# A third key buffer part, and one load for the second pair's keys, in a decode step of attention and MLP

## The chip, the cores and the metric

The kernel runs on one core of a Trainium2 chip. The time is device time in microseconds (us), from one launch; lower is better. A core has TensorE (PE, matmuls into the banks of PSUM), VectorE (DVE), ScalarE (ACT), GpSimd (POOL) and SyncE (SP, which here issues the transfers). Sixteen DMA engines carry the transfers between HBM and the on-chip memory SBUF, which has 128 partitions.

## The reference

One token (batch 1, sequence 1, width 512, bf16) goes through an attention block with a cache and then through an MLP block.

```
xn = layernorm(x)
q  = (xn @ wq) as 32 heads of 128
scores = q @ k_cache / sqrt(128)     # k_cache: 8 KV heads x 16384 positions x 128, 4 query heads per KV head
p  = softmax(scores);  o = p @ v_cache
h  = x + o @ wo
B(y): c  = gelu(layernorm(y) @ w1), four column groups shifted along the sequence, @ w2
      x1 = y + c
      return x1 + gelu(layernorm(x1) @ w3) @ w4
out = h + B(layernorm(h))
```

With a sequence of one token every shift by one or two positions brings in zeros, so w1 and w2 do not contribute and the kernel does not load them. k_cache and v_cache are 32 MB each, wq and wo 4 MB each, w3 and w4 1.75 MB each.

## The kernel before

Two KV heads form a pair; there are four pairs (PAIRS, 0 to 3). One pair's keys are 8 MB: 128 rows (partitions) of 64 KB; its values are as large. In SBUF `kb` holds one pair's keys, 64 KB per partition in two parts of 32 KB (`kb[0]`, `kb[1]`, the two halves of a pair); `vb` holds one pair's values, and wq before that. The weights wo go into `kb[0]`, w3 and w4 into `kb[1]`, once pair 3's keys have been used.

The chain of one pair: DVE transposes the first half of the keys from `kb` into `kt` (32 KB per partition) in blocks of 32x32 (L656), then the second half; PE multiplies each piece of `kt` with the queries `qn` into two banks of scores (L667); DVE takes the maximum (L681), PE and DVE make the bias from it, ACT writes exp of the scores into `p_sb` (L693), DVE transposes that into `pt` (L697), and PE multiplies `pt` with the values (L708). `kt` is reused piece by piece: a transpose of the second half waits until PE has read that piece of the first half. After pair 3 come the sum over heads, the product with wo (L794), the layernorm, w3 (L819), the gelu, w4 (L845) and the output's transfer.

What orders the work: every operation is appended to its engine's list in the order of the code and waits on semaphores for the operations that it depends on. Dependencies are named by keys. `("r", part, i)` stands for a key part: a load of the part writes it, so it waits until the transposes that read the part are done; `("kt", piece)` stands for a piece of the transposed keys; `"pt"` for the transposed probabilities. All large loads are issued by SyncE, in its list's order, and a load that waits holds up those behind it on that list. The values of the next pair are loaded into `vb` when PE has finished the pair's products (L708). The keys of the next pair are loaded by `load_keys(j, y)`: pairs in WHOLE in one load of 64 KB rows, the others in two loads of 32 KB rows, one for each half. CUTS and LAST cut the transposes of a half into pieces (five for a pair, nine for pair 3).

Of the kernel before, what the change touches and what calls it, by code (L numbers as in the profile page):

```python
# [349 lines left out]
D = 512  # L350
# [35 lines left out]
def bass_sequential_preLN__gqa_block_cached__mixer_s_mlp__decode_kernel(  # L386
# [13 lines left out]
    with ExitStack() as ctx:  # L400
# [30 lines left out]
        qcol = sb("qcol", [128, 4, PAIRS * REP, 32], FP32)  # L431
# [11 lines left out]
        osum = sb("osum", [128, D], FP32)  # L443
# [4 lines left out]
        hr = sb("hr", [128, 128], FP32)  # L448
        hx = sb("hx", [128, 128], FP32)
        rs = [sb(f"rs{i}", [128, 2], FP32) for i in range(2)]  # L450
        hc = sb("hc", [128, NCH, 32], BF16)
        xs = sb("xs", [128, 128], FP32)
        hg = sb("hg", [128, FQ], BF16)
        hT = sb("hT", [128, NCH, 32], FP32)
        hcol = sb("hcol", [128, NHC, 32], BF16)
        fin = sb("fin", [64, 256], BF16)
# [16 lines left out]
        def load(name, dst, src, key, by="SP", also=()):  # L473
            P.op(by, lambda e: e.dma_start(dst, src), w=[key, *also], dma=name)  # L474
# [12 lines left out]

        def load_values(j):
# [14 lines left out]
        def dve(fn, r=(), w=(), bank=(), own=None):  # L503
            return P.op("DVE", fn, r, w, bank, own=own)
# [24 lines left out]
        def piece(cuts, m):  # L529
            return [lo <= m < hi for lo, hi in cuts].index(True)  # L530
# [120 lines left out]
        def pieces(x, t, n):  # L651
            return x[:, :].rearrange("p (x l) -> p x l", x=2)[:, :, t * KP:(t + n) * KP]

        def transpose_keys(y, cuts):
            for t, n in zip(cuts, [b - a for a, b in zip(cuts, [*cuts[1:], 8])]):
                P.op("DVE", lambda e, t=t, n=n: e.transpose(pieces(kt, t, n).bitcast(I32), pieces(kb[y], t, n).bitcast(I32)),  # L656
                     r=[("r", y, i) for i in range(RPARTS)], w=[("kt", t + i) for i in range(n)], worth=n)
# [92 lines left out]
        for j in range(PAIRS):  # L750
            P.part()
            clear()
            P.part("query", j)
            dve(lambda e, j=j: e.tensor_copy(qn[:, :, :], qb[:, :, j, :]), r=["qb", ("s", 0), ("s", 1)], w=["qn"])
# [21 lines left out]
        act(lambda e: e.activation(scr[0:1, 1:2], mean4[0:1, 0:1], ACTF.Gelu_apprx_tanh), r=["mean4"], w=["scr"])  # L776
        for n, (lo, hi) in enumerate(WO):
            load(f"wo{n}", wo_sb[:, lo * D:hi * D], A_wo.rearrange("(p r) c -> p (r c)", p=128)[:, lo * D:hi * D],
                 ("r", 0, n))
        w3_in = B_w3.rearrange("(p k) f -> p k f", p=128)  # L780
        for n, (lo, hi) in enumerate(W3):
            load(f"w3{n}", w3_sb[:, lo:hi, :], w3_in[:, lo:hi, :], ("r", 1, n))
        w4_in = B_w4.rearrange("(p m) c -> p m c", p=128)
        for n, (lo, hi) in enumerate(W4):
            load(f"w4{n}", w4_sb[:, lo:hi, :], w4_in[:, lo:hi, :], ("r", 1, len(W3) + n))
# [4 lines left out]
        dve(lambda e: e.tensor_copy(o_b[:, :], o_f[:, :]), r=["o_f", ("r", 0, 0)], w=["o_b"])  # L790

        for r_ in range(32):
            q = r_ % 4
            pe(lambda e, r_=r_, q=q: e.matmul(O_ps[0][32 * q:32 * q + 32, :], copies(o_b[:, r_:r_ + 1], 32),  # L794
                                              wo_sb[:, r_ * D:(r_ + 1) * D], start=(r_ < 4),
                                              stop=(r_ < 4 or r_ >= 28), skip_group_check=(r_ >= 4)),
               r=["o_b"] + [("r", 0, n) for n in (piece(WO, r_),) if n], w=[("O", 0)], bank=[("O", 0)],
               times=None if r_ else 4, many=4)
        for n in range(2):
            unread(None)  # L800
# [4 lines left out]
        for q in range(4):  # L805
# [4 lines left out]
        S = ("st", 1)  # L810
        row_sums(1, h_ps, hkey)
        act(lambda e: e.activation(hc[:, :, :], hT[:, :, :], ACTF.Identity, bias=s[:, 0:1], scale=1.0),
            r=["hT", (S, 0)] + [("r", 1, 0)], w=["hc"])
        unread(4)


        for k in range(NCH):
            for q in range(4):
                pe(lambda e, k=k, q=q: e.matmul(s_ps[32 * q:32 * q + 32, 0, 0:FQ], hc[:, k, :],  # L819
                                                w3_sb[:, k, q * FQ:(q + 1) * FQ], start=(k == 0), stop=(k == NCH - 1)),  # L820
                   r=["hc"] + [("r", 1, n) for n in (piece(W3, k),) if n], w=[("s", 0)], bank=[("s", 0)])
# [5 lines left out]
        for n in range(2):  # L827
            lo, hi = n * NHC // 2, (n + 1) * NHC // 2
            act(lambda e, lo=lo, hi=hi: e.activation(
                hg[:, :].rearrange("p (i m) -> p i m", m=NHC)[:, :, lo:hi],  # L830
                s_ps[:, 0, 0:FQ].rearrange("p (i m) -> p i m", m=NHC)[:, :, lo:hi],
                ACTF.Gelu_apprx_tanh, scale=s[:, 7:8]), r=[("s", 0), (S, 7)], w=[("hg", n)], bank=[("s", 0)])
            dve(lambda e, lo=lo, hi=hi: e.transpose(
                hcol[:, lo:hi, :].rearrange("p m u -> p (m u)"),
                hg[:, :].rearrange("p (i m) -> p m i", m=NHC)[:, lo:hi, :]), r=[("hg", n)] + [("r", 1, len(W3))] * (n == 0), w=[("hcol", n)])
        for m in range(NHC):
            if m == 4:
                pe(None)
            if m == NHC - 1:
                for o in range(4):  # L840
                    pe(lambda e, o=o: e.ldweights(hcol[:, NHC - 1, :], tile_position=(0, 32 * o)), r=[("hcol", 1)])
            for o in range(4):
                pe(lambda e, m=m, o=o: held(
                    e, h_ps[32 * o:32 * o + 32, 0:128], hcol[:, m, :], w4_sb[:, m, o * 128:(o + 1) * 128], True)
                    if m == NHC - 1 else e.matmul(  # L845
                    h_ps[32 * o:32 * o + 32, 0:128], hcol[:, m, :], w4_sb[:, m, o * 128:(o + 1) * 128],
                    start=False, stop=False, skip_group_check=True),
                   r=[("hcol", 2 * m // NHC)] + [("r", 1, len(W3) + n) for n in (piece(W4, m),) if n],
                   w=[hkey], bank=[hkey])


# [38 lines left out]
```

## Time and profile before

| | before |
|---|---|
| time, median of 3 runs (lowest to highest) | 189.6 us (189.44 to 189.7) |
| span of the profiled execution, first to last instruction | 188.3 us |
| granted TensorE clock, mean over the span | 0.916 |
| bytes read from HBM | 79.17 MB, 420 GB/s over the span |
| key loads | 4 of 4 MB (32 KB rows), 2 of 8 MB (64 KB rows) |
| value loads | 4 of 8 MB |

The profiled execution's own time is its span; it leaves out what lies ahead of the first and behind the last instruction. If that execution took the median's time, this is 1.3 us. In the rows of the profile a line number is one of the code above, "out<-in" names the tiles, "x" counts instructions, and what stands behind an arrow in brackets ended the engine's idle time. SPq marks SyncE's issue of a transfer, which is not the transfer itself: "us to landing" runs from the issue to the last byte's arrival being told.

### The profile page before, as it was taken

The page shows a single profiled execution, that of the slowest core. Times are in us where ns is not written, and L with a number is a line of the kernel's source. Part 1 is how long each engine was busy: PE and PEld are TensorE (multiplying, and loading weights), DVE is VectorE, ACT ScalarE, POOL GpSimd, SP SyncE. Part 2 cuts the span into 40 slices and gives each one's busy share as a digit, 9 for nine tenths or more (in the row PEclk, how much of TensorE's full clock was granted, in tenths as well). Part 3 has the DMA queues.
Part 4 walks back from the last instruction along what each step waited for, and adds up shares of the span by engine and source line. Part 5 has one row for each costly group of instructions (what it writes and reads, how often), then busy time and mean ns, then how long its engine had stood idle before and what let it go on. Part 6 is the DMA issues. An engine that isn't in the chain of part 4 may idle for free.

```text
span 188.3 us, 2375 instructions
## 1 busy us (share of the span) xinstructions
PE 124.1 (66%) x760; PEld 48.3 (26%) x761; DVE 115.8 (62%) x138; ACT 13.7 (7%) x21; POOL 4.6 (2%) x8
## 2 busy tenths in 40 slices
PE   0109700698979978897910019799799889775772
PEld 0104200233322522332500003333244333222221
DVE  5730741999636998936300069993699898633173
ACT  3000200000004000004000000000400000500012
POOL 8100000000000000000000000000000000000000
PEclk9999985569999999999995557999999999999999
DMA  7999999999799999987999999998999996999994
GB/s 252 445 418 445 445 445 446 445 445 445 334 445 446 445 557 418 418 390 334 446 445 445 445 446 445 445 445 334 445 446 445 543 390 292 445 432 411 433 429 193
DMA packets 2607, 79.19 MB, mean 421 GB/s; under 512 B 302, under 2 KB 430, under 8 KB 686
## 3 DMA queue, kind: packets, MB, share of 16 engines
q1 hardware_dynamic: 2598, 79.17, 98.0%
q8 instruction: 1, 0.02, 0.0%
q10 hardware_dynamic: 8, 0.00, 0.0%
HBM read 79.17 MB, written 0.00 MB: 420 GB/s over the span
## 4 chain that ended last, share of the span: by engine, by line
DMA 69%; DVE 23%; PE 4%; issue 3%; SPq 1%; DVEq 0%
DMA kb<-in_A_k_cache_dram 54%; DVE kt L656 22%; DMA kb<-in_B_w_dram 15%; PE banks L667 3%; SPq L474 1%; PE banks L845 0%; DVE fin L852 0%; DVEq L147 0%; DVE den L725 0%; PE banks L524 0%; DVE od L723 0%; SPq L147 0%
## 5 line engine op out<-in xcount | busy, mean ns | idle before, releaser
L667 PE MATMUL banks<-kt,qn 128*128 x256 | 68.1, 401 | 36.8 <-DVE kt L656 35.7
L656 DVE STREAM_TRANSPOSE kt<-kb 128x2048 int32<-128x2048 int32 (+2 forms) x24 | 70.6, 2994 | 27.5 <-DMA kb<-in_A_k_cache_dram 26.4
L667 PEld LDWEIGHTS banks<-kt,qn 128*128 x256 | 25.4, 100 | 79.4 <-issue 65.5
L518 PE MATMUL banks<-qb 128*128 128x512 bf16 x61 | 22.1, 387 | 0.7 <-issue 0.2
L708 PE MATMUL banks<-vb,pt 128*32 128x512 bf16 x256 | 14.7, 379 | 1.1 <-POOLq L500 1.1
L693 ACT ACTIVATE p_sb<-banks,bias 128x1024 bf16<-128x1024 f32 x4 | 4.5, 1114 | 133.3 <-DVE nmh L688 133.3
L632 PE MATMUL banks<-vb,xn 128*128 x32 | 8.5, 432 | 6.7 <-DVE xn L623 6.7
L697 DVE STREAM_TRANSPOSE pt<-p_sb 64x1024 bf16<-64x1024 bf16 x8 | 9.9, 1239 | 4.4 <-ACT p_sb L693 4.3
L681 DVE TENSOR_REDUCE mx<-banks 128x1 f32<-128x1024 f32 x4 | 4.9, 1224 | 10.5 <-PE banks L667 10.5
L518 PEld LDWEIGHTS banks<-qb 128*128 128x128 bf16 x62 | 5.9, 97 | 16.0 <-issue 15.7
L708 PEld LDWEIGHTS banks<-vb,pt 128*32 128x32 bf16 x256 | 8.5, 97 | 5.4 <-POOLq L500 1.2
L639 DVE STREAM_TRANSPOSE qcol<-banks 64x1024 f32<-64x1024 f32 x4 | 4.8, 1227 | 6.7 <-PE banks L632 6.7
L632 PEld LDWEIGHTS banks<-vb,xn 128*128 128x128 bf16 x32 | 3.5, 108 | 11.4 <-issue 8.7
L676 ACT ACTIVATE banks<-mean 128x1024 f32<-128x1024 f32 x4 | 4.1, 1027 | 18.6 <-DVE qcol L639 18.5
L684 PE MATMUL banks<-mxd,mean 128*128 128x128 f32 x8 | 2.0, 326 | 4.7 <-DVE mxd L682 4.7
L732 DVE SCALAR_TENSOR_TENSOR od<-banks,rowc,od 128x128 f32<-128x128 f32 x12 | 4.2, 350 | 0.4
L794 PE MATMUL banks<-kb,o_b 128*32 128x512 bf16 x44 | 3.3, 384 | 1.6 <-DVE o_b L790 1.1
L729 DVE TENSOR_SCALAR od<-banks,rowc 128x128 f32<-128x128 f32 x4 | 1.3, 319 | 4.6 <-PE banks L708 4.6
L603 PE MATMUL banks<-x,quarter 4*128 4x128 bf16 x1 | 0.3, 286 | 5.4 <-DVE quarter L601 5.4
L601 DVE CAST quarter<-ident_f 4x128 bf16<-4x128 f32 x1 | 2.9, 2901 | 1.3 <-DMA x<-in_A_x_dram 1.3
L737 PE MATMUL banks<-od,zo 128*32 128x128 f32 x10 | 2.0, 283 | 1.8 <-DVE od L732 1.6
L803 DVE COPY osum<-banks 128x256 f32<-128x256 f32 x2 | 0.8, 418 | 4.0 <-PE banks L794 4.0
(74 smaller groups left out, 39.5 us busy)
## 6 DMA issues: line engine op xcount, KB each, us to landing
kb<-in_A_k_cache_dram SPq DMA_DIRECT2D x4, 4096.0 KB, 20.5
vb<-in_A_wq_dram SPq DMA_DIRECT2D x1, 3584.0 KB, 11.7
kb<-in_A_wo_dram SPq DMA_DIRECT2D x1, 2560.0 KB, 26.2
kb<-in_B_w_dram SPq DMA_DIRECT2D x1, 1792.0 KB, 24.4
kb<-in_A_wo_dram SPq DMA_DIRECT2D x1, 1536.0 KB, 29.5
kb<-in_B_w_dram SPq DMA_DIRECT2D x1, 1024.0 KB, 26.6
kb<-in_B_w_dram SPq DMA_DIRECT2D x1, 640.0 KB, 27.7
vb<-in_A_wq_dram SPq DMA_DIRECT2D x1, 512.0 KB, 3.6
```

The costliest lines, as they stand in the source:

```text
L518: P.op("PE", lambda e: e.matmul(O_ps[1][:, :], field[:, 0:128], field[:, 0:512], start=True, stop=True), r=["qb"], bank=[("O", 1)], times= ...
L632: pe(lambda e, k=k: e.matmul(row[:, bass.ds(P.b + P.b0, 512)], copies(xn[:, k:k + 1], 128), wq_k[:, k, bass.ds(P.c + P.c0, REP * DH)], sta ...
L639: dve(lambda e, g=g, b=b, half=half: e.transpose(qcol[64 * g:64 * g + 64, 2 * b:2 * b + 2, :, :].rearrange("p e m u -> p (e m u)"), half.r ...
L656: P.op("DVE", lambda e, t=t, n=n: e.transpose(pieces(kt, t, n).bitcast(I32), pieces(kb[y], t, n).bitcast(I32)), r=[("r", y, i) for i in ra ...
L667: pe(lambda e, n=n: e.matmul(row[:, bass.ds(P.y, 512)], qn[:, n, bass.ds(P.q, 128)], key_piece(P.k, n), start=False, stop=(n == 3), skip_g ...
L676: act(lambda e: e.activation(s_all, copies(mean4[:, 0:1], 1024), ACTF.Identity, scale=0.0), r=["mean4", "p"], w=[("s", 0), ("s", 1)], **both)
L681: dve(lambda e: e.tensor_reduce(mx[:, :], s_all, AX.X, ALU.max), r=[("s", 0), ("s", 1)], w=["mx"], **both)
L693: act(lambda e: e.activation(p_sb[:, :], s_all, ACTF.Exp, bias=bias[:, 0:1], scale=float(SCALE), accum_out=acc[:, :]), r=[("s", 0), ("s", ...
L697: dve(lambda e, g=g: e.transpose(pt[64 * g:64 * g + 64, :, :, g, :], p_sb[64 * g:64 * g + 64, :]), r=["p"], w=["pt"])
L708: pe(lambda e, l=l, ct=ct, ch=ch: e.matmul(O_ps[0][32 * ct:32 * ct + 32, :], pt[:, l, ch, :, :].rearrange("p g u -> p (g u)"), tiles[:, l ...
L732: dve(lambda e, block=block, c=c: e.scalar_tensor_tensor(od[:, :], block, rowc[:, c:c + 1], od[:, :], ALU.mult, ALU.add), r=[key, "rowc", ...
L794: pe(lambda e, r_=r_, q=q: e.matmul(O_ps[0][32 * q:32 * q + 32, :], copies(o_b[:, r_:r_ + 1], 32), wo_sb[:, r_ * D:(r_ + 1) * D], start=(r ...
```

## The change

`kb` gets a third part of 32 KB per partition. Pair 1's keys are now loaded whole, as pairs 0 and 2 are, and a table AT tells in which two neighbouring parts a whole load lands: pair 0 in parts 1 and 2, pair 1 in parts 0 and 1, pair 2 in parts 1 and 2. Pair 3's keys are still loaded by halves, into parts 0 and 1. The weights wo go into part 2, w3 and w4 into part 0. To make room, ten tiles that live only before, between or after the uses of `kt` become regions of `kt`: qcol, p_sb, osum, hg, hcol, fin, hc, hr, xs and hT. Since p_sb now lies in `kt`, the first key transpose of a pair also waits for `"pt"`, that is, for the operations that last wrote `pt`.

```
-WHOLE = (0, 2)
+WHOLE = (0, 1, 2)
+AT = (1, 0, 1)
...
-        p_sb = sb("p_sb", [128, 1024], BF16)
...
-        kb_all = sb("kb", [128, 256 * DH], BF16)
-        kb = [kb_all[:, i * 128 * DH:(i + 1) * 128 * DH] for i in range(2)]
+        kb_all = sb("kb", [128, 3 * 128 * DH], BF16)
+        kb = [kb_all[:, i * 128 * DH:(i + 1) * 128 * DH] for i in range(3)]
...
-        wq_sb, wo_sb = vb, kb[0]
-        w3_sb = kb[1][:, 0:NCH * FM].rearrange("p (k f) -> p k f", k=NCH)
-        w4_sb = kb[1][:, NCH * FM:2 * NCH * FM].rearrange("p (m c) -> p m c", m=NHC)
+        wq_sb, wo_sb = vb, kb[2]
+        w3_sb = kb[0][:, 0:NCH * FM].rearrange("p (k f) -> p k f", k=NCH)
+        w4_sb = kb[0][:, NCH * FM:2 * NCH * FM].rearrange("p (m c) -> p m c", m=NHC)
+        qcol = kt[:, 0:2 * 4 * PAIRS * REP * 32].bitcast(FP32).rearrange("p (b m u) -> p b m u", b=4, u=32)
+        p_sb = kt[:, 0:1024]
+        osum = kt[:, 0:2 * D].bitcast(FP32)
...
         def load_keys(j, y):
             n = 128 * DH
             if j in WHOLE:
-                load("k0", kb_all[:, :], pair_rows(A_k_cache, j), ("r", 0, 0),
-                     also=[("r", 0, i) for i in range(1, RPARTS)] + [("r", 1, i) for i in range(RPARTS)])
+                load("k0", kb_all[:, AT[j] * n:(AT[j] + 2) * n], pair_rows(A_k_cache, j), ("r", AT[j], 0),
+                     also=[("r", AT[j] + z, i) for z in range(2) for i in range(1 - z, RPARTS)])
                 return
-            load(f"k{y}", kb[y][:, :], pair_rows(A_k_cache, j)[:, y * n:(y + 1) * n], ("r", y, 0),
+            load(f"half{y}", kb[y][:, :], pair_rows(A_k_cache, j)[:, y * n:(y + 1) * n], ("r", y, 0),
                  also=[("r", y, i) for i in range(1, RPARTS)])
...
-        def transpose_keys(y, cuts):
+        def transpose_keys(y, cuts, at):
             for t, n in zip(cuts, [b - a for a, b in zip(cuts, [*cuts[1:], 8])]):
-                P.op("DVE", lambda e, t=t, n=n: e.transpose(pieces(kt, t, n).bitcast(I32), pieces(kb[y], t, n).bitcast(I32)),
-                     r=[("r", y, i) for i in range(RPARTS)], w=[("kt", t + i) for i in range(n)], worth=n)
+                P.op("DVE", lambda e, t=t, n=n: e.transpose(pieces(kt, t, n).bitcast(I32), pieces(kb[at], t, n).bitcast(I32)),
+                     r=[("r", at, i) for i in range(RPARTS)] + ["pt"] * (y == t == 0), w=[("kt", t + i) for i in range(n)], worth=n)
...
-                transpose_keys(y, LAST[y] if j == PAIRS - 1 else CUTS[y])
+                transpose_keys(y, *((LAST[y], y) if j == PAIRS - 1 else (CUTS[y], AT[j] + y)))
```

The remaining lines of the diff take the other tiles into `kt` in the same way and give the loads and uses of wo, w3 and w4 the keys of their new parts.

Two places show how this moves instructions. The first is SyncE's list, from the load of pair 0's values to that of wo. `kb` rows are keys (128x32768 is a whole load, 128x16384 a half, counted in bf16 elements), `vb` rows are values; in brackets stand the semaphores waited for: e_ those of an engine, d_ those of a load. Before:

```order
L474 DMA vb<-in_A_v_cache_dram 128x32768 [waits e_PE,e_DVE,d_wq1]
L474 DMA kb<-in_A_k_cache_dram 128x16384 [waits e_DVE,d_k0]
L474 DMA kb<-in_A_k_cache_dram 128x16384 [waits e_DVE]
L474 DMA vb<-in_A_v_cache_dram 128x32768 [waits e_PE,e_POOL_v,d_v]
L474 DMA kb<-in_A_k_cache_dram 128x32768 [waits d_k1,e_DVE,d_k0]
L474 DMA vb<-in_A_v_cache_dram 128x32768 [waits e_PE,e_POOL_v,d_v]
L474 DMA kb<-in_A_k_cache_dram 128x16384 [waits e_DVE,d_k0]
L474 DMA kb<-in_A_k_cache_dram 128x16384 [waits e_DVE]
L474 DMA vb<-in_A_v_cache_dram 128x32768 [waits e_PE,e_POOL_v,d_v]
L474 DMA kb<-in_A_wo_dram 128x10240 [waits e_DVE,d_k0]
```

And the same piece of the changed kernel:

```order
L474 DMA vb<-in_A_v_cache_dram 128x32768 [waits e_PE,e_DVE,d_wq1]
L474 DMA kb<-in_A_k_cache_dram 128x32768 [waits e_DVE,d_k0]
L474 DMA vb<-in_A_v_cache_dram 128x32768 [waits e_PE,e_POOL_v,d_v]
L474 DMA kb<-in_A_k_cache_dram 128x32768 [waits e_DVE,d_k0]
L474 DMA vb<-in_A_v_cache_dram 128x32768 [waits e_PE,e_POOL_v,d_v]
L474 DMA kb<-in_A_k_cache_dram 128x16384
L474 DMA kb<-in_A_k_cache_dram 128x16384 [waits e_DVE,d_k0]
L474 DMA vb<-in_A_v_cache_dram 128x32768 [waits e_PE,e_POOL_v,d_v]
L474 DMA kb<-in_A_wo_dram 128x10240 [waits e_DVE]
```

Pair 1's two halves have become one load, and the first half of pair 3's keys waits for nothing. The waits that keep their name have in part changed what they wait for: the one load for pair 1 (part 0 has never held keys, part 1 holds pair 0's first half) waits for the transposes of pair 0's first half; the load for pair 2 still waits for the transposes of pair 1's second half, which is now in part 1; the second half for pair 3 waits for those of pair 2's first half; wo waits for those of pair 2's second half, and w3 and w4 for those of pair 3's first half.

The second place is DVE's list around the turn from pair 0 to pair 1: the transposes into `pt`, the copy of the queries, and pair 1's key transposes. Before:

```order
L697 STREAM_TRANSPOSE pt<-p_sb 64x64x16 [waits e_POOL,e_ACT]
L697 STREAM_TRANSPOSE pt<-p_sb 64x64x16
L754 COPY qn<-qb 128x624 [waits e_ACT]
L656 STREAM_TRANSPOSE kt<-kb 128x2x1024 [waits d_k0]
L656 STREAM_TRANSPOSE kt<-kb 128x2x1024
L656 STREAM_TRANSPOSE kt<-kb 128x2x2048
L656 STREAM_TRANSPOSE kt<-kb 128x2x2048 [waits e_PE,d_k1]
L656 STREAM_TRANSPOSE kt<-kb 128x2x2048 [waits e_PE]
```

And in the changed kernel:

```order
L697 STREAM_TRANSPOSE pt<-kt 64x64x16 [waits e_ACT]
L697 STREAM_TRANSPOSE pt<-kt 64x64x16
L754 COPY qn<-qb 128x624 [waits e_ACT]
L656 STREAM_TRANSPOSE kt<-kb 128x2x1024 [waits e_DVE,d_k0]
L656 STREAM_TRANSPOSE kt<-kb 128x2x1024
L656 STREAM_TRANSPOSE kt<-kb 128x2x2048
L656 STREAM_TRANSPOSE kt<-kb 128x2x2048 [waits e_PE] x2
```

The first key transpose now also waits for DVE's own earlier work, and the second half's wait for a load of its own (d_k1) is gone. The order of the instructions is the same; so it is on PE, ACT and GpSimd.

More of the change, by code (lines that the diff above doesn't have):

```diff
@@ L447, in bass_sequential_preLN__gqa_block_cached__mixer_s_mlp__decode_kernel @@
         o_b = sb("o_b", [128, 32], BF16)
-        hr = sb("hr", [128, 128], FP32)
         hx = sb("hx", [128, 128], FP32)
         rs = [sb(f"rs{i}", [128, 2], FP32) for i in range(2)]
[L451 to L456, printed above, removed]
-        kb_all = sb("kb", [128, 256 * DH], BF16)
-        kb = [kb_all[:, i * 128 * DH:(i + 1) * 128 * DH] for i in range(2)]
+        kb_all = sb("kb", [128, 3 * 128 * DH], BF16)
+        kb = [kb_all[:, i * 128 * DH:(i + 1) * 128 * DH] for i in range(3)]
         vb = sb("vb", [128, 256 * DH], BF16)
         kt = sb("kt", [128, 128 * DH], BF16)
-        wq_sb, wo_sb = vb, kb[0]
-        w3_sb = kb[1][:, 0:NCH * FM].rearrange("p (k f) -> p k f", k=NCH)
-        w4_sb = kb[1][:, NCH * FM:2 * NCH * FM].rearrange("p (m c) -> p m c", m=NHC)
+        wq_sb, wo_sb = vb, kb[2]
[4 more added lines that the diff above has]
+        osum = kt[:, 0:2 * D].bitcast(FP32)
+        hg = kt[:, 2 * D:2 * D + FQ]
+        hcol = kt[:, 2 * D + FQ:2 * D + 2 * FQ].rearrange("p (m u) -> p m u", u=32)
+        fin = kt[0:64, 2048:2304]
+        hc = kt[:, 2304:2432].rearrange("p (k u) -> p k u", k=NCH)
+        hr, xs = (kt[:, at:at + 256].bitcast(FP32) for at in (2432, 2688))
+        hT = kt[:, 2944:3200].bitcast(FP32).rearrange("p (k u) -> p k u", k=NCH)
         banks = ps("banks", [128, 8, 512], FP32)
@@ L796, in bass_sequential_preLN__gqa_block_cached__mixer_s_mlp__decode_kernel @@
                                               stop=(r_ < 4 or r_ >= 28), skip_group_check=(r_ >= 4)),
-               r=["o_b"] + [("r", 0, n) for n in (piece(WO, r_),) if n], w=[("O", 0)], bank=[("O", 0)],
+               r=["o_b"] + [("r", 2, n) for n in (piece(WO, r_),) if n], w=[("O", 0)], bank=[("O", 0)],
                times=None if r_ else 4, many=4)
@@ L812, in bass_sequential_preLN__gqa_block_cached__mixer_s_mlp__decode_kernel @@
         act(lambda e: e.activation(hc[:, :, :], hT[:, :, :], ACTF.Identity, bias=s[:, 0:1], scale=1.0),
[L813 removed]
+            r=["hT", (S, 0)] + [("r", 0, 0)], w=["hc"])
         unread(4)
@@ L820, in bass_sequential_preLN__gqa_block_cached__mixer_s_mlp__decode_kernel @@
                                                 w3_sb[:, k, q * FQ:(q + 1) * FQ], start=(k == 0), stop=(k == NCH - 1)),
-                   r=["hc"] + [("r", 1, n) for n in (piece(W3, k),) if n], w=[("s", 0)], bank=[("s", 0)])
+                   r=["hc"] + [("r", 0, n) for n in (piece(W3, k),) if n], w=[("s", 0)], bank=[("s", 0)])
         act(lambda e: e.activation(xs[:, :], hr[:, :], ACTF.Identity, bias=s[:, 0:1], scale=1.0), r=["hr", (S, 0)], w=["xs"])
@@ L847, in bass_sequential_preLN__gqa_block_cached__mixer_s_mlp__decode_kernel @@
                     start=False, stop=False, skip_group_check=True),
-                   r=[("hcol", 2 * m // NHC)] + [("r", 1, len(W3) + n) for n in (piece(W4, m),) if n],
+                   r=[("hcol", 2 * m // NHC)] + [("r", 0, len(W3) + n) for n in (piece(W4, m),) if n],
                    w=[hkey], bank=[hkey])
```

12 lines of the change are left out of this document (5 added, 7 removed).

## The prediction, on record before the changed kernel was run

> **What bounds the kernel now.** I read the page first: engine shares, transfer queues, and which work ended last.
>
> ```profile
> PE 124.1 (66%) x760; PEld 48.3 (26%) x761; DVE 115.8 (62%) x138; ACT 13.7 (7%) x21; POOL 4.6 (2%) x8
> q1 hardware_dynamic: 2598, 79.17, 98.0%
> DMA 69%; DVE 23%; PE 4%; issue 3%; SPq 1%; DVEq 0%
> ```
>
> No engine is busy more than 66% of the span. The packets of SyncE's queue fill 98.0% of 16 engines' span of 188.3 us, that is 184.5 us. Next the chain of waits, in order of time (start, length), of which I take the transfers:
>
> ```profile
> 1.65 30.58 DMA kb<-in_A_k_cache_dram
> 50.18 20.82 DMA kb<-in_A_k_cache_dram
> 79.92 29.78 DMA kb<-in_A_k_cache_dram
> 158.53 27.68 DMA kb<-in_B_w_dram
> ```
>
> The ends of these pieces are landings: keys of pair 0 at 32.23, keys of pair 1 (second half) at 71.00, keys of pair 2 at 109.70, and the last but one piece of w4 at 186.21. Transfers run from about 1.75 to 186.2, 184.5 us, and their packets alone need 184.5. So the 16 engines work without a pause, and the chain's DVE and PE pieces only happen beside them. The tail is bound by the same transfers:
>
> ```profile
> 184.71 1.05 DVE L833 STREAM_TRANSPOSE hcol<-hg 128x224 bf16<-128x224 bf16 x2 [1.04 <-DMA kb<-in_B_w_dram]
> 186.26 0.46 PE L845 MATMUL banks<-kb,hcol 128*32 128x128 bf16 x20 [0.20 <-DMA kb<-in_B_w_dram]
> ```
>
> DVE and PE both stood waiting for w4 at the very end. Hence the rule for everything below: the end moves one for one with a pause in the transfer stream or with its rate, and by nothing else until more than 1.04 us is gained.
>
> Last, when SyncE issued each load (the timeline of its queue):
>
> ```profile
> 0.73 0.87 SPq L474 DMA_DIRECT2D vb<-in_A_wq_dram  x2
> 41.23 9.28 SPq L474 DMA_DIRECT2D kb<-in_A_k_cache_dram  x2
> 65.56 0.33 SPq L474 DMA_DIRECT2D vb<-in_A_v_cache_dram  x1
> 79.92 0.33 SPq L474 DMA_DIRECT2D kb<-in_A_k_cache_dram  x1
> 95.06 0.33 SPq L474 DMA_DIRECT2D vb<-in_A_v_cache_dram  x1
> 118.70 9.11 SPq L474 DMA_DIRECT2D kb<-in_A_k_cache_dram  x2
> 142.67 0.33 SPq L474 DMA_DIRECT2D vb<-in_A_v_cache_dram  x1
> 147.92 0.80 SPq L474 DMA_DIRECT2D kb<-in_A_wo_dram  x2
> 157.68 1.77 SPq L474 DMA_DIRECT2D kb<-in_B_w_dram  x4
> ```
>
> Each is issued well before the load ahead of it has landed. The closest is values 1 at 65.56, 5.4 us before keys 1 land at 71.00. That lead is what the change spends.
>
> **The change, part by part.**
>
> *One load of 64 KB rows for keys 1.* From 32.23 to 71.00, 38.77 us, the stream moved values 0 (8 MB, whole) and keys 1 (8 MB, two halves). From 71.00 to 109.70, 38.70 us, it moved values 1 and keys 2, both whole. So two halves cost 0.07 us more than a whole load, and the term is **-0.07 us**. Everything later inherits it.
>
> *Loads that can be issued earlier.* The first half of keys 3 now follows values 2 on SyncE with no wait, its second half needs the first half of pair 2's transposes instead of the second, and wo, w3 and w4 each wait half a pair less. All are queued some 10 us and more ahead of their turn in the rows above, in a stream without pauses: **0**. The cover is that stream; without it each would be worth what its lead lacks, and none lacks any.
>
> *Where keys 1 land.* Before, the first half landed early and pair 1's transposes began at once:
>
> ```profile
> kb<-in_A_k_cache_dram SPq DMA_DIRECT2D x1, 4096.0 KB, 20.1
> 32.33 8.83 DVE L656 STREAM_TRANSPOSE kt<-kb 128x2048 int32<-128x2048 int32 x3 [6.36 <-DMA kb<-in_A_k_cache_dram]
> 41.38 8.77 DVE L656 STREAM_TRANSPOSE kt<-kb 128x4096 int32<-128x4096 int32 x2 [0.23 <-PE banks L667]
> 61.38 8.83 DVE L656 STREAM_TRANSPOSE kt<-kb 128x2048 int32<-128x2048 int32 x3
> 71.09 8.77 DVE L656 STREAM_TRANSPOSE kt<-kb 128x4096 int32<-128x4096 int32 x2 [0.88 <-DMA kb<-in_A_k_cache_dram]
> 109.79 17.66 DVE L656 STREAM_TRANSPOSE kt<-kb 128x2048 int32<-128x2048 int32 x5 [18.82 <-DMA kb<-in_A_k_cache_dram]
> 34.00:35.00 1.00, 0.19 (x1) 0.14 (x2) 1.00 (x2) 0.00 (x0) 0.00 (x0) 0.50 1.21 524
> 112.00:113.00 1.00, 0.72 (x2) 0.35 (x3) 1.00 (x2) 0.00 (x0) 0.00 (x0) 0.50 0.00 0
> ```
>
> The half issued at 41.23 took 20.1 us, so it landed at 61.3, and DVE started at 61.38. Pair 1 ended its transposes at 79.86, and keys 2 were issued at 79.92. Now both halves land together at 71.00 - 0.07 = 70.93. Pair 1 becomes like pairs 0 and 2, whose five transposes begin 0.09 to 0.10 us after the landing and take 17.66 us (pair 2) or, with the 0.23 us in which DVE waited for PE, 50.15 - 32.33 = 17.82 us (pair 0). PE's clock adds nothing beyond this: both pairs began with PE at half clock (0.50 in the third column from the end of the two windows). They end at 88.69 to 88.85. Keys 2 go into parts 1 and 2, and part 1 holds the second half of keys 1, so this load waits for the last of these transposes as it did before. It is **issued at 88.75 to 88.91** instead of 79.92. Behind it on SyncE stand values 2 and, through them, all the rest.
>
> When does the stream need it? Packets show by their starts (columns ahead of the end: granted clock, DMA share, GB/s):
>
> ```profile
> 87.50:89.40 1.90, 1.85 (x6) 0.48 (x5) 1.26 (x2) 1.62 (x3) 0.00 (x0) 1.00 0.00 0
> 89.40:89.90 0.50, 0.50 (x2) 0.10 (x2) 0.50 (x1) 0.00 (x0) 0.00 (x0) 1.00 4.86 2097
> vb<-in_A_v_cache_dram SPq DMA_DIRECT2D x1, 24.8
> ```
>
> 2097 GB/s in 0.50 us is 1.05 MB: sixteen packets of 64 KB, one on each engine, the first of keys 2. So values 1 leave the engines between 89.40 and 89.90 (their landing is told at 65.56 + 24.8 = 90.36, some 0.46 us after). In the changed kernel these are 89.33 to 89.83.
>
> How long from issue to first packet? The trace has it only for an empty queue, at the start and for the output:
>
> ```profile
> 0.73:1.68 0.95, 0.00 (x0) 0.00 (x0) 0.18 (x3) 0.37 (x1) 0.72 (x3) 1.00 0.00 0
> 1.75:2.10 0.35, 0.00 (x0) 0.00 (x0) 0.00 (x0) 0.35 (x1) 0.35 (x1) 1.00 1.39 189
> 187.14 0.32 SPq L855 DMA_DIRECT2D out_dram<-fin  x1
> 187.25:187.85 0.60, 0.00 (x0) 0.00 (x0) 0.00 (x0) 0.00 (x0) 0.00 (x0) 0.60 0.00 0
> vb<-in_A_wq_dram SPq DMA_DIRECT2D x1, 512.0 KB, 3.6
> ```
>
> The output's packets begin after 187.85, 0.71 us or a little more behind its issue; the first load's begin at about 1.75, 1.02 us behind it, and spread over 0.35 us. So the first packets of keys 2 come at 88.75 + 0.71 = 89.46 at best and 88.91 + 1.02 + 0.35 = 90.28 at worst. Against the last engine's 89.83 that is no pause at best and 0.45 us at worst. An engine that has run dry may also need time to come to its rate. The first load shows the most: 3.6 us, less 1.02 to its first packet, less 1.21 for 512 KB at 19.35 us per 8 MB, less 0.46 to be told, leaves 0.9. So the pause costs **0 to 1.35 us**. I take **+0.2**: the middle issue, 88.83, and the middle delay, 0.87, give 89.70, 0.12 behind the middle engine's 89.58, and a small part of the 0.9, because the engines are still busy when the load comes, which is nearer to a filled queue than to the program's start.
>
> The Trainium skill, "DMA: Bandwidth & Descriptors", section Specifications, gives about 0.6 us to the first byte of a load issued from SyncE; by that the packets come at 89.4 to 89.5, there is no pause, and the sum would be -0.07. Both of this trace's rows are longer than that.
>
> *Short-lived tiles in the transposed keys' tile.* The instructions keep their shapes, so their durations. The one new wait is DVE's on its own transposes of p ahead of each pair's first key transpose. Between them stands the copy of qn, 0.32 us, and then the wait for the keys; so **0**. Were that cover gone, the price would be that of DVE ops that wait for the op ahead, 8.30 and 8.49 below, about 0.03 us a pair. For pair 0 it is GpSimd's memset, done at 5.31 and needed at 32.3. Queued behind are only that pair's transposes.
>
> ```profile
> 8.30 0.16 DVE L577 SCALAR_TENSOR_TENSOR st<-st 128x1 f32<-128x1 f32 x1
> 8.49 0.16 DVE L578 SCALAR_TENSOR_TENSOR sti<-st,sti 128x2 f32<-128x2 f32 x1
> 61.06 0.32 DVE L754 COPY qn<-qb 128x624 bf16<-128x624 bf16 x1
> 3.51 1.80 POOL L609 MEMSET pt<- 128x2048 bf16 x1
> ```
>
> *What follows in pair 1.* Pair 2 took 142.67 - 109.70 = 32.97 us from its keys' landing to the issue of the next values. So values 2 are issued at 70.93 + 32.97 = 103.9 instead of 95.06, more than 5 us before keys 2 leave the engines at about 109.2. Pair 2 and all behind it run as before, shifted.
>
> **Sum.** -0.07 + 0.2 = +0.13 us on a span of 188.3: 188.4. The median of the three runs is 189.6, so 1.3 us lie around the profiled span; I add them: **189.7 us**.
>
> **The rivals.**
>
> *The load is in time.* Keys 2 come within the lead and nothing pauses: -0.07, 189.5 us. For it: the output's 0.71 us, and leads that were always enough. Against: every earlier lead was above 5 us, this one is 0.5 to 1.1 us.
>
> *The queue runs dry (slower).* Place: SyncE's issue of keys 2 after pair 1's last transpose. It decides from the point where the first packet comes later than the last engine is free, 89.83. Price: 0.45 us of pause and up to 0.9 us to fill again, so +0.5 to +1.3 net, 190.1 to 190.9, about 190.2 if half the filling time shows. For it: the first load's 1.02 us. Against: the engines are not cold.
>
> *Faster.* After 129 us the stream is a little slower than before: values 3 landed at 142.67 + 25.4 = 168.07 (its row gives 25.4) and keys 3 at 148.57, so 19.50 us against 19.35. If issues in the midst of the stream cost that, the earlier issues could return some 0.15 for each of values 3, keys 3 and wo, 0.45 in all: 189.1. Nothing in the trace ties it to the issues.
>
> ```profile
> vb<-in_A_v_cache_dram SPq DMA_DIRECT2D x1, 25.4
> kb<-in_A_k_cache_dram SPq DMA_DIRECT2D x1, 4096.0 KB, 21.1
> ```
>
> (The second row is the last half of keys 3, issued at 127.47.) A fixed cost of a load is its stronger form: 3.6 - 1.21 = 2.4 us of the first load are not movement, and one load fewer would give 187.2; but the two halves lost 0.07, so it lies hidden. The skill's same page, section "Anatomy of one DMA", puts some 2.0 us on each load from GpSimd, which would give 187.6.
>
> **How the numbers follow.** Within 0.2% is 0.38 us, about what can be told from no change. Forecast, a pause of 0.1 to 0.45 us: 0.36. In time: 0.28. Dry queue: 0.25. Faster by earlier issues: 0.09, by a fixed cost: 0.02. The first two lie within the bound, so same is about 0.63 (0.01 of their edge to the slower side), slower 0.26, faster 0.11. The range reaches from 189.3, between the load in time and the faster case, to 190.4, beyond the middle of the dry queue. The likeliest case's own range is 189.5 to 189.9.
>
> **What would show it.** Pair 1's first transpose at 71.0 and its last end at 88.7 to 88.9; keys 2 issued right after; a stretch with no packet starts near 89.5 to 90 if the queue paused; keys 2 landed at 109.6 (in time), 109.8 (forecast) or after 110.1 (dry). I am wrong if the transposes take longer than 17.9 us, if values 2 come late, or if the loads after 129 us change their pace.

## The result and the profile after

The changed kernel takes 190.99 us (median of 6 runs, 190.41 to 192.47) against 189.66 us before on the same chip (6 runs, 189.44 to 189.89). The ratio is 1.0082, with a 95% interval of 1.0063 to 1.0101: slower by 1.3 us. The runs also spread by 2.1 us, those of the kernel before by 0.45.

The profiled execution of the changed kernel took 190.43 us, its span is 189.1, so 1.3 us lie around it, as assumed. It is one of the two fastest of its runs, and its profile shows less than the median lost. The page, engine shares, queue and who ended last:

```profile
PE 125.1 (66%) x760; PEld 48.6 (26%) x761; DVE 116.2 (61%) x138; ACT 13.7 (7%) x21; POOL 4.6 (2%) x8
q1 hardware_dynamic: 2454, 79.17, 97.5%
DMA 79%; DVE 19%; SPq 1%; issue 0%; PE 0%; DVEq 0%
```

The engines' work is what it was. The same bytes fill 97.5% of a longer span, 184.4 us against 184.5: over the whole span the packets took no more time. (At one place they did, as is seen below; the other stretches together took about as much less.) Where the new time lies is seen in the chain of waits of the changed kernel (start, length):

```profile
41.22 29.73 DMA kb<-in_A_k_cache_dram
88.72 22.01 DMA kb<-in_A_k_cache_dram
149.71 37.32 DMA kb<-in_B_w_dram
```

Keys 1 land at 70.95 (71.00 before), keys 2 at 110.73 (109.70 before), the last but one piece of w4 at 187.03 (186.21 before). Between keys 1 and keys 2 the stream carries two whole loads, which took 38.70 us before and now take 39.78. That is a loss of 1.08 us in one place; 0.05 came in ahead of it, and from keys 2 to w4 the stream takes 76.30 us instead of 76.51. The sum, 1.08 - 0.05 - 0.21 = 0.82, is the span's 189.1 - 188.3 = 0.8.

DVE's and SyncE's timeline around that place:

```profile
71.03 17.61 DVE L656 STREAM_TRANSPOSE kt<-kb 128x2048 int32<-128x2048 int32 x5 [9.81 <-DMA kb<-in_A_k_cache_dram]
88.72 0.33 SPq L474 DMA_DIRECT2D kb<-in_A_k_cache_dram  x1
103.84 0.33 SPq L474 DMA_DIRECT2D vb<-in_A_v_cache_dram  x1
104.22 15.82 SPq L474 DMA_DIRECT2D kb<-in_A_k_cache_dram  x2
```

Pair 1's transposes wait 9.81 us for the one load, run from 71.03 to 88.64, and keys 2 are issued behind them at 88.72. The packets (windows; the last two columns are DMA share and GB/s, by the packets' starts):

```profile
87.50:89.40 1.90, 1.58 (x7) 0.71 (x8) 1.83 (x5) 0.00 (x0) 0.00 (x0) 1.00 0.00 0
89.40:89.75 0.35, 0.35 (x3) 0.00 (x0) 0.32 (x2) 0.00 (x0) 0.00 (x0) 1.00 0.02 0
89.75:90.65 0.90, 0.90 (x5) 0.38 (x4) 0.33 (x1) 0.00 (x0) 0.00 (x0) 1.00 3.28 1165
90.65:92.65 2.00, 2.00 (x9) 0.77 (x8) 0.00 (x0) 0.00 (x0) 0.00 (x0) 1.00 0.00 0
```

1165 GB/s in 0.90 us are sixteen packets of 64 KB, the first of keys 2. They start 1.03 to 1.93 us behind the issue, where before they followed between 89.40 and 89.90 without a pause. And they are long: a share of 3.28 on 16 engines over 0.90 us is 47.2 us, 2.95 us for each, where 4.86 over 0.50 us was 2.43 before. The middle of the starts, 90.2, lies 0.55 us behind that of before, 89.65. So about 0.5 us of pause and 0.5 us of slow first packets make up the loss.

### The profile page after: what moved, and what is told of

Same layout as the page of the kernel before. It is cut to its first block, busy times and chain, and to the rows that moved or that the text cites. A ratio compares the mean times of both kernels' runs of the same rounds, so it can differ in the third digit from the quotient of the medians.

```text
span 189.1 us, 2372 instructions
## 1 busy us (share of the span) xinstructions
PE 125.1 (66%) x760; PEld 48.6 (26%) x761; DVE 116.2 (61%) x138; ACT 13.7 (7%) x21; POOL 4.6 (2%) x8
## 3 DMA queue, kind: packets, MB, share of 16 engines
q1 hardware_dynamic: 2454, 79.17, 97.5%
## 4 chain that ended last, share of the span: by engine, by line
DMA 79%; DVE 19%; SPq 1%; issue 0%; PE 0%; DVEq 0%
DMA kb<-in_A_k_cache_dram 59%; DMA kb<-in_B_w_dram 20%; DVE kt L656 19%; SPq L474 1%; PE banks L845 0%; DVE kt L852 0%; DVEq L147 0%; PE banks L524 0%; SPq L147 0%; DVE den L725 0%
## 5 line engine op out<-in xcount | busy, mean ns | idle before, releaser
L667 PE MATMUL banks<-kt,qn 128*128 x256 | 68.8, 405 | 36.6 <-DVE kt L656 35.4
L693 ACT ACTIVATE kt<-banks,bias 128x1024 bf16<-128x1024 f32 x4 | 4.5, 1116 | 134.0 <-DVE nmh L688 134.0
L697 DVE STREAM_TRANSPOSE pt<-kt 64x1024 bf16<-64x1024 bf16 x8 | 9.9, 1239 | 4.4 <-ACT kt L693 4.3
L639 DVE STREAM_TRANSPOSE kt<-banks 64x1024 f32<-64x1024 f32 x4 | 4.8, 1227 | 6.9 <-PE banks L632 6.9
L803 DVE COPY kt<-banks 128x256 f32<-128x256 f32 x2 | 0.8, 419 | 4.0 <-PE banks L794 4.0
```

The costliest lines, as they stand in the source:

```text
L639: dve(lambda e, g=g, b=b, half=half: e.transpose(qcol[64 * g:64 * g + 64, 2 * b:2 * b + 2, :, :].rearrange("p e m u -> p (e m u)"), half.r ...
L667: pe(lambda e, n=n: e.matmul(row[:, bass.ds(P.y, 512)], qn[:, n, bass.ds(P.q, 128)], key_piece(P.k, n), start=False, stop=(n == 3), skip_g ...
L693: act(lambda e: e.activation(p_sb[:, :], s_all, ACTF.Exp, bias=bias[:, 0:1], scale=float(SCALE), accum_out=acc[:, :]), r=[("s", 0), ("s", ...
L697: dve(lambda e, g=g: e.transpose(pt[64 * g:64 * g + 64, :, :, g, :], p_sb[64 * g:64 * g + 64, :]), r=["p"], w=["pt"])
```

## The experiments

The theory: the loss comes from the load of keys 2 being issued late, because it waits for pair 1's last transpose. Its rivals: the third part and the tiles in `kt` cost the time; pair 1's whole load, or pair 1's work coming later, costs it in another way. Every kernel below computes the whole result.

All losses in the stream are worked out as above: from the landing of keys 1 to that of keys 2, less 38.70 us. The landings are the ends of pieces in each profile's chain of waits.

**The change once more**, on one chip with the next two kernels and with the first set of runs at 88.2.

> The changed kernel once more, beside the others on one chip. Late load (theory): keys 2 are issued at 88.7 after pair 1's last transpose, their first packets start 1.0 us later, after values 1 have left all engines, and are stretched; keys 2 land about 20.4 us after values 1 instead of 19.35; 190.4 to 191.5 us, runs spread by 1 us or more. Rival, that the third part or the tiles in kt cost the time: the same time, but the loss would be spread over the pairs and not stand at keys 2 alone.

190.92 us (190.69 to 191.79; before 189.53; ratio 1.0066, 1.0053 to 1.0079). Its profiled execution was the slowest of these runs: keys 2 issued at 89.04, landing at 111.54, a loss of 1.57 us at the same place. It also lost 0.3 us ahead of keys 1 (71.27) and 0.4 behind keys 2 (76.70 us to w4), so not all of the spread between runs lies at keys 2.

**Pair 1 in halves again, all the rest kept.**

```
-WHOLE = (0, 1, 2)
+WHOLE = (0, 2)
```

> The change with pair 1's keys again in two loads of 32 KB rows (WHOLE = (0, 2)); third part, earlier issues of keys 3, wo, w3 and w4, and the tiles in kt are kept. Late load: pair 1's transposes begin at 61.4 and end at 79.9, keys 2 are issued at 79.9, nothing pauses: 189.3 to 189.8 us, spread within 0.5. Tiles in kt or third part as the cause: 190.5 to 191.5, as with the change. If the earlier issues return time, 189.1 to 189.3.

189.43 us (11 runs, 189.37 to 189.90; ratio 0.9997, 0.9988 to 1.0006). The transposes begin with the first half again, keys 2 are issued at 79.91:

```profile
61.35 8.83 DVE L656 STREAM_TRANSPOSE kt<-kb 128x2048 int32<-128x2048 int32 x3 [0.17 <-DMA kb<-in_A_k_cache_dram]
71.06 8.77 DVE L656 STREAM_TRANSPOSE kt<-kb 128x4096 int32<-128x4096 int32 x2 [0.88 <-DMA kb<-in_A_k_cache_dram]
41.17 29.81 DMA kb<-in_A_k_cache_dram
79.91 29.77 DMA kb<-in_A_k_cache_dram
```

From 70.98 to 109.68 are 38.70 us: no loss. So the third part, ten tiles in `kt`, DVE's new wait and all the earlier issues together neither cost nor bring more than the 0.2 us that the interval leaves open; the merge costs it all.

**Pair 1 whole, but the wait taken away by another place.** Pair 2's keys go into parts 0 and 2, by one load with 32 KB rows on the SBUF side, so that the load needs the transposes of pair 1's first half only. Pair 3's halves go into parts 1 and 0, w3 and w4 into part 1.

```
-AT = (1, 0, 1)
+PART = ((1, 2), (0, 1), (0, 2), (1, 0))
...
+                lo, hi = PART[j]
+                dst, src = kb_all[:, lo * n:(hi + 1) * n], pair_rows(A_k_cache, j)
+                if hi - lo == 2:
+                    dst = kb_all[:, :].rearrange("p (x l) -> p x l", x=3)[:, 0:3:2, :]
+                    src = src.rearrange("p (x l) -> p x l", x=2)
```

> The change with pair 1's keys still whole, but pair 2 put into parts 0 and 2, so that its load waits for the transposes of pair 1's first half and not for the last one. Late load: keys 2 are issued at about 79.9 although pair 1's transposes end at 88.7; no pause; 189.3 to 189.8 us, spread within 0.5. If the whole load of pair 1, or pair 1's work coming 9 us later, costs the time in another way: 190.4 to 191.5, as with the change.

189.52 us (12 runs, 189.34 to 190.22; ratio 1.0006, 0.9996 to 1.0015). The spread is 0.9 us instead of the 0.5 expected, by one run of 190.22 that was not profiled. Timeline, windows and chain:

```profile
70.93 17.68 DVE L662 STREAM_TRANSPOSE kt<-kb 128x2048 int32<-128x2048 int32 x5 [9.79 <-DMA kb<-in_A_k_cache_dram]
79.84 0.62 SPq L474 DMA_DIRECT2D kb<-in_A_k_cache_dram  x1
87.50:89.30 1.80, 1.58 (x8) 0.74 (x8) 1.74 (x4) 0.00 (x0) 0.00 (x0) 1.00 0.00 0
89.30:89.90 0.60, 0.60 (x4) 0.12 (x2) 0.55 (x2) 0.00 (x0) 0.00 (x0) 1.00 2.04 874
41.15 29.71 DMA kb<-in_A_k_cache_dram
79.84 29.82 DMA kb<-in_A_k_cache_dram
```

Pair 1's work is as late as in the changed kernel, keys 2 are issued at 79.84, and their sixteen packets (now 32 KB) start between 89.30 and 89.90. Keys 1 land at 70.86, keys 2 at 109.66: 38.80 us, 0.10 more than two loads of 64 KB rows. That is about what the two halves of pair 1 cost (38.77 to 38.80 us for values 0 and keys 1 in the kernel before and with pair 1 in halves), though it is a single load: what the merge saves seems to go with the packets of 32 KB and not with the number of loads.

**The same with the wait put back.** Nothing but one dependency is added, on the last piece of pair 1's transposes.

```
-                     also=[("r", lo, i) for i in range(1, RPARTS)] + [("r", hi, i) for i in range(RPARTS)])
+                     also=[("r", lo, i) for i in range(1, RPARTS)] + [("r", hi, i) for i in range(RPARTS)], after=[("kt", 7)] * (j == 2))
```

(`after` is a new argument of `load`: keys that the load waits for without using them.)

> The kernel with pair 1 whole and pair 2 in parts 0 and 2, which lost nothing, with one more wait: the load of keys 2 waits for pair 1's last transpose although its parts are free. Late load: issue at 88.7 again, loss back, 190.4 to 191.5 us as with the change. If the place of pair 2's keys in the buffer was what helped: 189.3 to 189.8.

190.73 us (190.63 to 191.31; before 189.56; ratio 1.0070, 1.0056 to 1.0084).

```profile
88.69 0.62 SPq L474 DMA_DIRECT2D kb<-in_A_k_cache_dram  x1
41.26 29.71 DMA kb<-in_A_k_cache_dram
88.69 22.31 DMA kb<-in_A_k_cache_dram
90.05:90.65 0.60, 0.60 (x4) 0.20 (x3) 0.05 (x1) 0.00 (x0) 0.00 (x0) 1.00 3.24 874
```

70.97 to 111.00 are 40.03 us: a loss of 1.33. The first sixteen packets start 1.4 to 2.0 us behind the issue, and each takes 1.94 us (3.24 x 16 x 0.60 / 16) instead of the 1.22 of the run above. The time of the issue alone, 79.84 or 88.69, makes the difference of these two kernels. With that the theory stands and the rivals fall.

What was left was the price, since the loss was larger than forecast. For that the kernel before was given one more wait, so that its load of keys 2 is issued later and later, with pair 1 in halves and no third part:

```
-                if j < PAIRS - 1 and (y or j + 1 not in WHOLE):
+                if j < PAIRS - 1 and (y or j + 1 not in WHOLE) and j != 1:
                     load_keys(j + 1, y)
...
             softmax(j)
+            if j == 1:
+                load_keys(2, 1, after=["mx"])
             unread(14)
```

(`load_keys` hands `after` on to `load`.) The key in `after` differs: "mx" (pair 1's maximum), "o_m" (the spread of pair 0's output), "p" (exp), "p" and a small ScalarE operation behind it (of 8 or of 256 columns), the first transpose of p, "pt" (both).

**Issued at 85.4.**

> The kernel before, the load of keys 2 also waits for pair 1's maximum: issue at about 85.45, 4.0 us before the first engine is free (89.45). Late load with a delay of 1.0 to 3.0 us to the first packets, as in the runs with a pause: packets ready by 88.5, no pause, 189.4 to 189.8 us. If a load issued within the last round of 64 KB packets (from 84.6) is always slow to start, 190.5 or more.

189.44 us (10 runs; before 189.48; ratio 1.0003, 0.9992 to 1.0014).

```profile
50.01 20.97 DMA kb<-in_A_k_cache_dram
85.40 24.28 DMA kb<-in_A_k_cache_dram
158.43 27.56 DMA kb<-in_B_w_dram
87.50:89.50 2.00, 1.94 (x6) 0.48 (x5) 1.37 (x2) 1.61 (x3) 0.00 (x0) 1.00 0.00 0
89.50:89.85 0.35, 0.35 (x2) 0.10 (x1) 0.35 (x1) 0.00 (x0) 0.00 (x0) 1.00 6.94 2996
```

70.98 to 109.68: 38.70 us, nothing lost with a lead of about 4 us. Its third row answers another question: from keys 2 to w4, landing at 185.99, it takes 76.31 us, as in the changed kernel (76.30), though it issues keys 3, values 3 and the weights as late as the kernel before. In the other late runs of this kernel whose chain shows it, this stretch takes 76.26 to 76.34 us. So the 0.2 us that the changed kernel won there are not due to its earlier issues; it is the one profile of the kernel before that is long there.

**Issued at 87.1.**

> The kernel before, the load of keys 2 also waits for the spread of pair 0's output: issue at about 87.1, 2.35 us before the first engine is free. Delay of 1.0 to 3.0 us: ready at 88.1 to 90.1, so 0 to 0.5 us lost, 189.5 to 190.2. If only an issue after the engines are dry costs anything, 189.4 to 189.8; if the loss at 88.16 was peculiar to what ran beside it, also 189.4 to 189.8.

190.53 us (189.57 to 190.82; ratio 1.0046, 1.0031 to 1.0061): already 1.0 us lost, more than the 190.2 that was expected at most. The profiled execution is the fastest of these runs and shows only the edge of it:

```profile
50.03 20.97 DMA kb<-in_A_k_cache_dram
87.07 22.79 DMA kb<-in_A_k_cache_dram
87.50:89.35 1.85, 1.79 (x6) 0.42 (x5) 1.23 (x1) 1.62 (x3) 0.00 (x0) 1.00 0.00 0
89.35:89.90 0.55, 0.55 (x2) 0.14 (x2) 0.54 (x2) 0.00 (x0) 0.00 (x0) 1.00 4.62 1907
```

All sixteen packets start on time, yet they take 4.62 x 16 x 0.55 / 16 = 2.54 us each instead of 2.43, and 71.00 to 109.86 are 38.86 us. The longer runs of this kernel were not profiled, so where they lost the rest is not shown.

**Issued at 88.2, twice.**

> The kernel before with one more wait and nothing else: the load of keys 2 also waits for pair 1's exp, which puts its issue at about 88.1 instead of 79.9. Late load: first packets at 89.1 to 89.9 against engines free at 89.4 to 89.9, so a loss of 0.2 to 1.0 us, 189.9 to 190.7, and runs that spread more than those of the kernel before. Cause in the merge, the parts or the tiles: none of them is here, so 189.5 to 189.8.

192.03 us (191.56 to 192.76; before 189.53; ratio 1.0133, 1.0113 to 1.0153), well above the 190.7 that was expected at most.

```profile
50.18 20.85 DMA kb<-in_A_k_cache_dram
88.16 23.70 DMA kb<-in_A_k_cache_dram
```

From 71.03 to 111.86, a loss in the stream of 2.13 us: more than the changed kernel, with an issue half a microsecond earlier. Hence once more, with a point between:

> The kernel before with keys 2 waiting for pair 1's exp, once more (issue about 88.1). If a lead of 1.3 us really costs more than one of 0.7 us: 191.6 to 192.8 us, keys 2 landing 21.2 us or more after values 1. If the first time was chance: 190.7 to 191.3, as with issues at 88.6 to 89.4.

191.32 us (191.06 to 192.35; before 189.52; ratio 1.0090, 1.0074 to 1.0107). The profiled execution is its slowest:

```profile
50.07 20.98 DMA kb<-in_A_k_cache_dram
88.17 24.47 DMA kb<-in_A_k_cache_dram
87.75:89.75 2.00, 1.94 (x6) 0.47 (x6) 1.56 (x2) 1.42 (x3) 0.00 (x0) 1.00 0.00 0
89.75:90.40 0.65, 0.65 (x2) 0.18 (x2) 0.65 (x1) 0.00 (x0) 0.00 (x0) 1.00 3.00 1210
90.40:91.15 0.75, 0.72 (x3) 0.19 (x2) 0.59 (x2) 0.00 (x0) 0.00 (x0) 1.00 0.00 0
91.15:91.85 0.70, 0.70 (x15) 0.43 (x18) 0.00 (x0) 0.00 (x0) 0.00 (x0) 1.00 1.17 374
```

In this profile the engines are free between 89.8 and 90.15. Twelve of them (1210 GB/s x 0.65 us) begin keys 2 then, eleven at once. The other four (374 x 0.70) begin only at 91.15 to 91.85, 3.0 to 3.7 us behind the issue. By the packets of the trace these four finish keys 2 at 112.0 to 112.3, the twelve by 110.8, and the landing is told at 112.64. So the four set the loss of 2.89 us (71.05 to 112.64).

**Issued at 88.5 and at 88.6.**

> The kernel before, keys 2 also wait for a very small extra ScalarE operation behind pair 1's exp (0.2 us): issue at about 88.35. Between the points at 88.16 (192.0) and 88.60 (191.1): 191.1 to 191.9 if the cost falls evenly as the issue comes later; near 191.0 if 88.16 was chance.

The extra operation (8 columns in the first, 256 in the second; nothing reads its result):

```
             if j == 1:
+                act(lambda e: e.activation(later[:, :], copies(mean4[:, 0:1], 8), ACTF.Identity, scale=0.0),
+                    r=["mean4", "p"], w=["later"])
+                load_keys(2, 1, after=["later"])
```

The first took 191.57 us (190.52 to 191.86; before 189.52; ratio 1.0090, 1.0055 to 1.0125); a loss of 2.20 us in the profiled execution (71.12 to 112.02):

```profile
50.14 20.98 DMA kb<-in_A_k_cache_dram
88.47 23.55 DMA kb<-in_A_k_cache_dram
```

> The kernel before, the load of keys 2 also waits for a small extra ScalarE operation behind pair 1's exp (0.5 us, its result is not used), so that it is issued at about 88.7, at the changed kernel's time but with pair 1 in halves. If the loss depends on the lead alone: 190.4 to 191.5, less than at 88.16. If it depends on what pair 1 is doing beside it (here the transposes of p, in the changed kernel the scores): 191.5 to 192.8, as at 88.16.

The second took 191.06 us (190.87 to 191.47; before 189.56; ratio 1.0086, 1.0070 to 1.0101); a loss of 1.54 us (71.03 to 111.27):

```profile
50.07 20.96 DMA kb<-in_A_k_cache_dram
88.60 22.67 DMA kb<-in_A_k_cache_dram
```

At the changed kernel's time of issue the kernel before loses what the changed kernel loses, though DVE transposes p beside it there, and PE does scores in the other. So what pair 1 does at that time doesn't matter much.

**Issued at 89.4, as the engines run dry.** The first of the two transposes of p gets a key of its own. (Two semaphore increments behind the loads of values, SEEN and ROUND, also go up by one, from 53 and 28 to 54 and 29.)

```
-                    r=["p"], w=["pt"])
+                    r=["p"], w=["pt"] + ["pt0"] * (g == 0))
```

> The kernel before, the load of keys 2 also waits for the first of pair 1's two transposes of p: issue at about 89.45, just as the first engine runs dry. Lead alone, with packets 1.0 us behind the issue: 0.8 us of pause and 0.5 of stretch, 190.7 to 191.3. If the delay is 1.3 to 3.0 us as at 88.16: 191.8 to 193.

190.94 us (190.85 to 191.49; before 189.56; ratio 1.0081, 1.0066 to 1.0097); a loss of 1.60 us (70.98 to 111.28).

```profile
50.02 20.96 DMA kb<-in_A_k_cache_dram
89.38 21.90 DMA kb<-in_A_k_cache_dram
```

**Issued when all engines are dry.** Keys 1 landed 0.5 us late in this profile, so the engines were free between 90.2 and 90.6, and the issue is at 91.15.

> The kernel before, the load of keys 2 also waits for pair 1's transposes of p: issue at about 90.7, 0.8 us after the last engine has run dry. If the slow start comes from engines that are still busy, the first packets come 1.0 to 1.4 us after the issue as at the program's start, 2.1 to 2.4 us lost and some 0.5 for stretched packets: 192.0 to 192.6. If a late load always needs up to 3.0 us to reach all engines: 193 to 194.

192.39 us (192.13 to 192.58; before 189.48; ratio 1.0139, 1.0122 to 1.0156).

```profile
50.02 21.49 DMA kb<-in_A_k_cache_dram
91.15 21.75 DMA kb<-in_A_k_cache_dram
88.20:92.10 3.90, 3.81 (x20) 1.14 (x23) 2.80 (x3) 1.43 (x3) 0.00 (x0) 1.00 0.00 0
92.10:92.40 0.30, 0.30 (x12) 0.20 (x5) 0.00 (x0) 0.00 (x0) 0.00 (x0) 1.00 9.21 3058
92.40:93.10 0.70, 0.70 (x20) 0.49 (x15) 0.00 (x0) 0.00 (x0) 0.00 (x0) 1.00 0.48 187
```

Fourteen packets (3058 x 0.30) start 0.95 to 1.25 us behind the issue, two more within 1.95. They take 3.10 us on average ((9.21 x 0.30 + 0.48 x 0.70) x 16 / 16); the loss is 2.69 us (71.51 to 112.90). The runs spread by only 0.45 us, the least of the late ones.

Together (lead: from the issue to 89.4, when the first engine is free, in single profiles the stream ran up to 0.6 us later, and the lead is longer by that; for the dry case to 90.2; loss in the profiled execution; median less that of the kernel before on the same chip):

| kernel | issue of keys 2 | lead | loss in the stream | median, less before |
|---|---|---|---|---|
| before | 79.92 | 9.5 | 0 (the measure) | 0 |
| pair 2 in parts 0 and 2 | 79.84 | 9.6 | 0.10 | 0.0 |
| pair 1 in halves | 79.91 | 9.5 | 0.00 | -0.1 |
| before, late | 85.40 | 4.0 | 0.00 | 0.0 |
| before, late | 87.07 | 2.3 | 0.16 | +1.0 |
| before, late | 88.16, 88.17 | 1.2 | 2.13, 2.89 | +2.5, +1.8 |
| before, late | 88.47 | 0.9 | 2.20 | +2.0 |
| before, late | 88.60 | 0.8 | 1.54 | +1.5 |
| parts 0 and 2, wait back | 88.69 | 0.7 | 1.33 | +1.2 |
| the change | 88.72, 89.04 | 0.7 | 1.08, 1.57 | +1.3, +1.4 |
| before, late | 89.38 | 0.0 | 1.60 | +1.4 |
| before, late | 91.15 | -0.9 | 2.69 | +2.9 |

How late the last of the sixteen engines begins keys 2 can be read from the packets of each trace. Behind the issue it was 3.0 and 3.7 us for the issues at 88.2, 3.2 at 88.5, 2.5 at 88.6, 2.0 with the wait put back, 1.9 and 2.3 for the change, 2.1 at 89.4 and 1.9 with all engines dry. A lead of 4.0 us is longer than the longest of these and one of 2.3 is not, which would explain what these two leads cost; this is argued, as the longer runs at 2.3 were not profiled.

No version beat the kernel before: the two that repair the change are level with it.

## Why the prediction was wrong, point by point

*What bounds the kernel* was right: the transfer stream had no pause, and the span moved one for one with one that was made (1.08 lost at keys 2, 0.82 in the span after what was won elsewhere).

*One load of 64 KB rows, -0.07 us*: values 0 and keys 1 took 70.95 - 32.24 = 38.71 us instead of 38.77 (the chain's first transfer ends at 32.24), so -0.06.

*Loads that can be issued earlier, 0*: right, by the kernel with pair 1 in halves, which has them all and is at 0.9997. The rival *faster by earlier issues* falls with the same run, and with the one issued at 85.4, which wins the same 0.2 us behind keys 2 without them. The rival of a fixed cost for each load, forecast at -2.4 us, falls too: one load fewer brought 0.06.

*Where keys 1 land*: forecast were transposes from 71.0 to 88.69 or later, the issue of keys 2 at 88.75 to 88.91 and of values 2 at 103.9; measured were 71.03 to 88.64, 88.72 (0.03 ahead of the forecast's early end) and 103.84.

*Short-lived tiles and DVE's new wait, 0*: right, by the same run as above.

*The pause, 0 to 1.35 us, taken at +0.2*: **this step failed**, and it is a term whose mechanism was named and whose size was wrong. It measured 1.08 and 1.57 us in the two profiles of the change, and about 1.4 in the median (1.33 slower, 0.07 won by the merge). The rival *the queue runs dry* is what happened; it was given a chance of 0.25 and 190.1 to 190.9 us, and the median came out just above it. Both parts of the term were sized wrong.

First, the delay from issue to first packet was bounded by rows of an empty queue, 0.71 and 1.02 us with a spread of 0.35, so 1.37 us at worst, and taken at 0.87. Measured were 1.03 to 1.93 us in the changed kernel, and 3.0 to 3.7 us for four engines of one run. An empty queue doesn't bound it either: at dry engines the last packet started up to 1.95 us behind the issue.

Second, the time to come to the full rate was bounded by 0.9 us, which held for the changed kernel (0.5 us: 2.95 less 2.43). But only "a small part" of it was taken, by the sentence that the engines are still busy when the load comes, "which is nearer to a filled queue than to the program's start". The runs show no such gain. The first packets were slow in the profile of every load issued at 88.16 or later, those issued into a running stream (2.95 us in the changed kernel) as well as those at dry engines (3.10). Nor did the running stream make the start more even: at dry engines 14 of 16 engines began within 0.95 to 1.25 us, and the least even starts are those at leads of 0.9 to 1.2 us. The last engine sets the landing, so an uneven start costs as much as its slowest engine.

The rule that followed, no pause as long as the first packet comes before the last engine is free, would have put the decision point at a lead of 0.3 to 0.9 us on the scale of the table, which counts to the first engine, some 0.45 us ahead of the last. By the runs it lies between 2.3 us, where 1.0 us is lost, and 4.0 us, where nothing is.

The page of the Trainium skill that was weighed there ("DMA: Bandwidth & Descriptors", Specifications, about 0.6 us to the first byte) erred to the same side; the least that a run here shows for keys 2 is about 0.95 us. The same page of the Trainium skill, section "Latency and other measured facts", puts HBM's access latency at 0.2 us on average and 2 us at high load. Starts of up to 3.7 us in the running stream, against 1.95 at dry engines, would go in that direction; no run here shows in which part of the way the time goes.

The range was too narrow even by the prediction's own bounds: 189.6 - 0.07 + 1.35 is 190.9, and it ended at 190.4. The sums of the rival that should have stretched it are off as well. With 0.45 us of pause, half the filling time and the 0.07 won it comes to 189.6 + 0.45 + 0.45 - 0.07 = 190.4, not 190.2, and 190.4 is not beyond the middle of 190.1 to 190.9.

## What to carry to other kernels

Before two loads are merged, ask what starts with the first half's landing: here one merge saved 0.06 us in the stream and moved the end of pair 1's transposes, and with it the issue of the next load, by 8.8 us. In a kernel that lives by its transfers, read each load's lead, from its issue to the moment when the queue ahead of it runs out; here 4.0 us were enough and 2.3 were not. If a buffer's place makes a load wait for the last use of the data ahead, another place can give the lead back at no cost, as pair 2 in parts 0 and 2 did.

## What the runs showed of the hardware that was not expected

A late load does not cost the less, the earlier it comes: with leads of 0.7 to 1.2 us the median lost 1.2 to 2.5 us, with a lead of 0 only 1.4. The two sets of runs at the lead of 1.2 differ among themselves (1.0113 to 1.0153 and 1.0074 to 1.0107), so the shape between 0 and 1.2 us is not settled, only that a loss is there throughout. Nor is the slow start of the first packets in proportion to their bytes: it added 0.5 us to packets of 64 KB in the changed kernel and 0.7 to packets of 32 KB with the wait put back, and in the changed kernel the packets behind them are at 2.42 us again.

Why some engines begin 3 us and more behind the issue, while twelve of the sixteen begin at once or nearly so, stays open, and so does why the first packets are slow. It also stays open why the runs of the change and of the leads of 0.9 to 2.3 us spread by 1.1 to 2.1 us, where those of the other late kernels spread by 0.45 to 0.7 and those of the kernel before stay within 0.6.
